# An attention level cut into a state step and a chunk step, in a fused attention and two-MLP kernel

## The chip, the cores and the metric

The kernel runs on one core of one Trainium2 chip. The metric is the device time of one launch in microseconds (us), as the median of several executions. The engines are called as in the profile: PE is TensorE's matmul, PEld its weight load, DVE is VectorE, ACT is ScalarE, POOL is GpSimd and SP is the engine that issues most DMAs.

## The reference

A gated linear attention over 4 batches, 8 heads and 768 positions (head size 32, state size 16) feeds two MLPs over 3072 tokens of width 256 and hidden width 2048.

```python
for c in range(nc):                      # chunks of the sequence
    cum = np.cumsum(la, axis=-1)         # la: log of the decays a
    M = einsum('bhin,bhjn->bhij', Cc, Bc) * exp(cum_i - cum_j) * causal
    y_intra = einsum('bhij,bhjd->bhid', M, xc)
    y_inter = einsum('bhin,bhnd->bhid', Cc, state) * exp(cum)
    y[:, :, sl] = y_intra + y_inter
    state = decay_full * state + sum_j(Bc * xc * decay_from_j)
...
x = relu(x @ w_in) ** 2 @ w_out          # first MLP
h = x @ w2_in
out = (h * clip(h + 3, 0, 6) / 6) @ w2_out
```

## The kernel before

The kernel is written with a manual schedule: each engine executes its instructions in the order in which the code emits them, and waits where an operand is not there yet.

The attention is cut into 12 levels of 64 positions. A level needs, on PE: `scores` (C times B for each head, 16 matmuls as written), `inter` (the state times C, 32 matmuls of 32 columns of weights each), `update` (the new contribution to the state, 16) and `intra` (the masked scores times x, 32). All four are in fp32, and each such matmul as written shows in the profile as two matmuls and two weight loads. They use one PSUM tile `att` per level, of which there is only one buffer. `phase(l)` emits, in one go, the scores of level l+1 and then inter, update and intra of level l. On the other engines a level has: `scale` (POOL, B and C times decays, L289), `heads` (ACT, the operand `cb` of the scores, L298), `tokens` (POOL, L304), `mask` (DVE, L323, reads the scores), `advance` (DVE, the next state S, L374 and L376, reads the part `u` of `att` that update wrote), `evac_h` (ACT, L389, the high part of the result, `act_h`) and `evac_l` (DVE, L394, the low part, `act_l`).

Levels 0 and 1 are done before the first MLP begins. The rest is done between the steps of the first MLP. There are 96 steps; a step takes one block of 128 hidden units for 512 tokens: `mm1` (6 matmuls into `ha`, L516), then a gate (relu on ACT, a square on ACT or a product on DVE, the high part `gha` on ACT, the low part `gla` on DVE), and the `mm2` (6 matmuls into `ya`, L550) of two steps before. `ORDER` gives the steps: tile 0 with 10 blocks, tile 1 with 10 blocks, then the rest. So step 10 is the first that needs the results of levels 2 and 3.

The table `PLAN` says which attention work is emitted in which step: for level l, phase in step 4l-5, then mask, advance, tokens and evac_h in step 4l-4, evac_l and scale in step 4l-3, heads in step 4l-2. Work on PE stands between `mm1` and `mm2` of its step, the other work after ACT's `gha` of its step. In the same steps the weights of the first MLP are decoded (`early` on ACT L433, `join` on DVE L437 to L447, `split` on ACT L474 and POOL L476, by the table `JOIN1`). The table `SQUARE` lists the steps whose square ACT does instead of DVE. `gammas` multiplies the decays of the later levels (3 instructions, in step 2). `keep_busy` issues dummy matmuls. Later come the second MLP's steps, from the line L656 on.

Of the kernel before, what the change touches and what calls it, by code (L numbers as in the profile page):

```python
# [8 lines left out]
F32 = mybir.dt.float32  # L9
# [5 lines left out]
ALU = mybir.AluOpType  # L15
# [3 lines left out]
P = 128  # L19
# [29 lines left out]
ORDER += [(t, f) for t in range(2, NT) for f in range(NF)]  # L49


PLAN = {0: ["adv1", "upd1", "head2"], 1: ["first2", "tok2", "scale3"], 2: ["mask2", "head3", "gammas0"]}
for _l in range(2, 12):
    for _k, _v in ((-1, ("load",)), (0, ("phase",)), (1, ("mask+", "adv", "tok+", "high")), (2, ("low", "scale++")),
                   (3, ("head++",))):
        PLAN.setdefault(4 * _l - 5 + _k, []).extend(
            f"{v.rstrip('+')}{_l + v.count('+') + 2 * (v == 'load')}" for v in _v)

JOIN1 = {0: 3, 1: 4, 2: 5, 3: 6, 5: 7, 6: 8, 7: 9, 10: 10, 11: 11, 14: 12, 15: 13, 18: 14, 19: 15}
DMA1 = {0: 6, 1: 7, 2: 8, 3: 9, 5: 10, 6: 11, 10: 12, 11: 13, 14: 14, 15: 15}

SQUARE = (1, 2, 3, 4, 5, 7, 8, 9, 10, 12, 14, 16, 18, 20)
QKEEP = 3
QNEW = 4

# [8 lines left out]
def attn_mlp_mlp(ctx: ExitStack, tc, a, bT, cT, bK, x, w1i, w1o, w2i, w2o, yT):  # L76
# [153 lines left out]
                          .unsqueeze(1).broadcast_to([H, NS, 2 * NGRP * CPG]))  # L230

    def gammas():
        nc.vector.tensor_tensor(out=gl[:, 1, :, 0:NLEV - 1], in0=gl[:, 1, :, 0:NLEV - 1], in1=gl[:, 0, :, 1:NLEV],
                                op=ALU.mult)
        for e in range(2):
            nc.vector.tensor_scalar(out=gam1[:, :, :, e].rearrange("p l b -> p b l"), in0=gl[:, 1, :, CPG - 1:NLEV - 1],
                                    scalar1=hm[:, e:e + 1], scalar2=None, op0=ALU.mult)

    def gamma(l):
        return gam0[:, l] if l < CPG - 1 else gam1[:, l - CPG + 1]  # L240
# [66 lines left out]
    def scores(l, sc):  # L307

        d = lev[l]
        d["s"] = sc  # L310
        for c in range(2):
            for p in range(NPR):
                for r in range(2):
                    q, b = slice(32 * p, 32 * p + 32), 2 * r + c
                    nc.tensor.matmul(out=sc[CH * r:CH * r + CH, p, P * c:P * c + P].rearrange("j (e i) -> j e i", e=2),  # L315
                                     lhsT=d["bc"][q, b, 1], rhs=d["cb"][q, :, b], start=True, stop=True)
# [7 lines left out]
                                      tri.bitcast(U32).unsqueeze(1).unsqueeze(1).broadcast_to([P, 2, NB, CH]),  # L324
                                      sc[:, q].rearrange("p k (z i) -> p k z i", i=CH))

    def inter(l, m=HD):

        y, d = lev[l]["y"], lev[l]
        for b in range(NB):  # L330
            for p in range(NPR):
                q, (r, c) = slice(32 * p, 32 * p + 32), divmod(b, 2)
                for e in range(0, 2 * HD, m):
                    o = CH * (p % 2) + e
                    nc.tensor.matmul(out=y[o:o + m, 2 * r + p // 2, c * CH:c * CH + CH],  # L335
                                     lhsT=state["S"][q, b, e:e + m], rhs=d["bc"][q, b, 0], start=c == 0,
                                     stop=False, skip_group_check=True)

    def intra(l):

# [13 lines left out]
    def update(l):  # L354

        if l == NLEV - 1:
            return
        u, x = lev[l]["u"], lev[l]["xb"]
        for c in range(2):
            for r in range(2):  # L360
                q = slice(CH * r, CH * r + CH)
                for p in range(NPR):
                    nc.tensor.matmul(out=u[32 * p:32 * p + 32, 2 * r, 2 * HD * c:2 * HD * c + 2 * HD],
                                     lhsT=x[q, c, DM + 32 * p:DM + 32 * p + 32], rhs=x[q, c, 64 * p:64 * p + 64],
                                     start=not l, stop=True, skip_group_check=True)
# [28 lines left out]
            nc.vector.tensor_tensor(out=lo, in0=outputs(l, r), in1=hi.bitcast(F32), op=ALU.subtract)  # L394

    def place(l, t):
        lev[l].update(t=t, y=t[:, :, G:G + P], u=t[:, :, G + P:])

    def phase(l):
        t = ps_a.tile([P, NPR, TOK], F32, tag="att", name=f"att{l}")  # L400
        place(l, t)
        if l + 1 < NLEV:
            scores(l + 1, t[:, :, 0:G])
        inter(l)
        update(l)
        intra(l)


    class Weights:
# [313 lines left out]
    def run(g, point):  # L723
        for f in jobs.pop((g, point), ()):
            f()
# [88 lines left out]
    ftps = ps_a.tile([P, NPR, TOK], F32, tag="att", name="ftp")  # L814
    f_tokens(0)
    f_tokens(1)
    keep_busy(4, ftps[:, 2])
    gammas_out()
    decays_out()
    gammas_in()  # L820
# [24 lines left out]
    update(0)  # L845
    keep_busy(2, lev[0]["t"][:, 3, 0:G], G)
    intra(0)
    load_x(3)
    advance(0)
    evac_h(0)  # L850
    evac_l(0)
    place(1, ps_a.tile([P, NPR, TOK], F32, tag="att", name="att1"))
    inter(1, 2 * HD)
    intra(1)
    w1.sign(1)
    w1.bits(1)
    evac_h(1)
# [12 lines left out]
    def first_scores(l):  # L870
        sc = ps_a.tile([P, NPR, TOK], F32, tag="att", name=f"att_s{l}")
        scores(l, sc[:, :, 0:G])

    does = {"load": load_all, "scale": scale, "head": heads, "tok": tokens, "first": first_scores, "mask": mask,
            "phase": phase, "high": evac_h, "low": evac_l, "upd": update, "adv": advance, "gammas": lambda _: gammas()}

    def attention(n, on_pe):
        for nm in PLAN.get(n, ()):
            k = nm.rstrip("0123456789")
            l = int(nm[len(k):])  # L880
            if (k in ("phase", "first", "upd")) == on_pe and (l < NLEV or k in ("load", "scale", "head")):
                does[k](l)

    todo = {}
# [14 lines left out]
            w1.early(plan[f + 1])  # L899

    def mid(n):
        attention(n, False)
        decode(JOIN1, n)
        if n in DMA1:
            w1.dma(DMA1[n])
        run(n, 0)


    for q, base in enumerate((48, 54, 60, 66, 72, 79, 86, 91)):
# [88 lines left out]
```

## Time and profile before

| | us |
|---|---|
| median of 3 runs (592.23 to 594.0) | 593.2 |
| the profiled execution, its own time | 590.14 |
| its span in the profile | 588.4 |
| PE busy | 557.6 |
| DVE busy | 420.8 |
| ACT busy | 361.1 |
| POOL busy | 141.7 |

The span is the time from the first to the last instruction of the profiled execution, and its own time is that with what lies around it. A busy share is an average over the whole span; which engine waits for which has to be read stretch by stretch.

### The profile page before, as it was taken

How to read it: one execution, taken by the hardware profiler on the slowest of the kernel's cores; microseconds unless marked ns; L12 is line 12 of the kernel's file. 1: busy time of each engine (PE TensorE's matmuls, PEld its weight loads, DVE VectorE, ACT ScalarE, POOL GpSimd, SP SyncE). 2: the span in 40 equal slices, each digit the busy share in tenths (PEclk: the TensorE clock that was granted, in tenths of full speed). 3: DMA queues.
4: the chain of work that ended last, by engine and by line, in shares of the span. 5: the costliest groups of instructions: out<-in, count | busy, mean ns of one | idle time of the engine just before them, and what ended most of it. 6: DMA issues, size and time to landing. Idle time of an engine off the chain costs nothing.

```text
span 588.4 us, 11061 instructions
## 1 busy us (share of the span) xinstructions
PE 557.6 (95%) x4451; PEld 450.4 (77%) x4451; DVE 420.8 (72%) x662; ACT 361.1 (61%) x629; POOL 141.7 (24%) x195
## 2 busy tenths in 40 slices
PE   7879998888899999999999899999999999999996
PEld 3557876777688888888887678888788888788885
DVE  6889787455654576677777877788776878777674
ACT  4567865443434556656665776687766777666663
POOL 5355443510000134444346500330000510000000
PEclk9789999999989999999999999999999999999999
DMA  8895442212000111222121000000200000200002
GB/s 245 210 263 139 125 135 81 78 37 90 1 2 1 36 43 65 73 71 72 41 66 38 1 1 0 1 1 1 72 1 0 1 2 0 71 2 0 1 1 72
DMA packets 26467, 31.47 MB, mean 53 GB/s; under 512 B 2128, under 2 KB 21040, under 8 KB 26416
## 3 DMA queue, kind: packets, MB, share of 16 engines
q1 hardware_dynamic: 24544, 29.85, 18.3%
q10 hardware_dynamic: 1872, 0.92, 0.6%
q8 instruction: 35, 0.57, 0.4%
q14 instruction: 16, 0.13, 0.1%
HBM read 27.41 MB, written 3.35 MB: 52 GB/s over the span
## 4 chain that ended last, share of the span: by engine, by line
PE 81%; issue 5%; POOL 4%; DVE 4%; DMA 2%; ACT 2%; SPq 1%; POOLq 0%; DVEq 0%; ACTq 0%
PE y L701 22%; PE ya L550 18%; PE ha L516 17%; PE X L656 11%; PE Z L656 6%; PE V L656 3%; PE att L349 1%; PE att L335 1%; POOL al L476 1%; PE att L315 1%; POOL bc L289 1%; DMA bc<-in_bT 1%; DMA gsc<-gs 1%; POOL wtb L456 1%; POOL bl L502 1%
## 5 line engine op out<-in xcount | busy, mean ns | idle before, releaser
L533 DVE TENSOR_TENSOR gla<-ga,gha 128x512 fp32r<-128x512 f32 x96 | 75.9, 791 | 41.0 <-ACT gha L531 40.5
L523 ACT ACTIVATE ga<-ha 128x512 f32<-128x512 f32 x96 | 57.3, 597 | 68.1 <-PE ha L516 67.8
L531 ACT ACTIVATE gha<-ga 128x512 fp32r<-128x512 f32 x96 | 60.6, 631 | 53.5 <-DVE ga L529 53.2
L529 DVE TENSOR_TENSOR ga<-ga,ha 128x512 f32<-128x512 f32 x82 | 56.2, 685 | 45.7 <-ACT ga L523 45.3
L550 PE MATMUL ya<-gla,ah 128*128 128x512 f32 x192 | 75.7, 394 | 1.4 <-DVE gla L533 1.4
L516 PE MATMUL ha<-act_h,ah 128*128 128x512 f32 x192 | 76.2, 397 | 0.7 <-ACT act_h L389 0.7
L550 PE MATMUL ya<-gha,ah 128*128 128x512 f32 x192 | 76.4, 398 | 0.2 <-ACT gha L531 0.2
L516 PE MATMUL ha<-act_h,al 128*128 128x512 f32 x192 | 75.7, 394 | 0.0
L550 PE MATMUL ya<-gha,al 128*128 128x512 f32 x192 | 75.3, 392 | 0.0
L516 PE MATMUL ha<-act_l,ah 128*128 128x512 f32 x192 | 75.2, 393 | 0.0
L687 DVE TENSOR_TENSOR glc<-c,ghc 128x512 fp32r<-128x512 f32 x96 | 67.6, 706 | 5.9 <-ACT ghc L684 4.7
L678 DVE SCALAR_TENSOR_TENSOR c<-rc,c 128x512 f32<-128x512 f32 x72 | 51.0, 708 | 23.7 <-ACT rc L670 23.4
L670 ACT ACTIVATE rc<-c,three 128x512 f32<-128x512 f32 x72 | 52.0, 722 | 24.5 <-DVE c L665 24.3
L701 PE MATMUL y<-ghc,bh 128*128 128x512 f32 x168 | 65.5, 390 | 0.0
L701 PE MATMUL y<-glc,bh 128*128 128x512 f32 x168 | 65.4, 389 | 0.0
L701 PE MATMUL y<-ghc,bl 128*128 128x512 f32 x168 | 65.4, 389 | 0.0
L684 ACT ACTIVATE ghc<-c 128x512 fp32r<-128x512 f32 x96 | 58.6, 629 | 3.4 <-DVE c L678 3.2
L665 DVE TENSOR_TENSOR c<-Z,u 128x512 f32<-128x512 f32 x48 | 33.1, 690 | 22.9 <-PE Z L656 22.1
L550 PEld LDWEIGHTS ya<-gla,ah 128*128 128x128 f32 x192 | 36.3, 189 | 10.6 <-DVE gla L533 3.1
L550 PEld LDWEIGHTS ya<-gha,ah 128*128 128x128 f32 x192 | 36.2, 189 | 10.4 <-issue 2.0
L516 PEld LDWEIGHTS ha<-act_h,ah 128*128 128x128 f32 x192 | 36.7, 191 | 8.9 <-ACT act_h L389 1.0
L661 ACT COPY u<-X 128x512 f32<-128x512 f32 x48 | 28.2, 588 | 24.4 <-PE X L656 24.3
(299 smaller groups left out, 1037.4 us busy)
## 6 DMA issues: line engine op xcount, KB each, us to landing
rawa<-in_w1i SPq DMA_DIRECT2D x8, 512.0 KB
rawa<-in_w1o SPq DMA_DIRECT2D x8, 512.0 KB
rawb<-in_w2i SPq DMA_DIRECT2D x8, 512.0 KB
rawb<-in_w2o SPq DMA_DIRECT2D x8, 512.0 KB
xb<-in_x SPq DMA_DIRECT2D x24, 128.0 KB
ef<-scr SPq DMA_DIRECT2D x10, 256.0 KB
out_yT<-xf SPq DMA_DIRECT2D x10, 256.0 KB
bc<-in_cT SPq DMA_DIRECT2D x6, 256.0 KB
```

Source lines behind the costliest of these rows:

```text
L516: nc.tensor.matmul(out=h, lhsT=wt[fb][:, k, fo * P:fo * P + P], rhs=xt[t][:, k, :], start=i == 0, stop=i == 5)
L523: nc.scalar.activation(out=g, in_=h, func=AF.Relu)
L529: nc.vector.tensor_tensor(out=g, in0=g, in1=h, op=ALU.mult)
L531: nc.scalar.activation(out=gh, in_=g, func=AF.Copy)
L533: nc.vector.tensor_tensor(out=gl, in0=g, in1=gh.bitcast(F32), op=ALU.subtract)
L550: nc.tensor.matmul(out=ys[m], lhsT=terms[i][0][fb][:, fo, m * P:m * P + P], rhs=terms[i][1], start=first and i == 0, stop=last and i == 2)
L656: nc.tensor.matmul(out=self.ps[bank], lhsT=lhsT, rhs=rhs, start=start and i == 0, stop=stop and i == 2, skip_group_check=True)
L670: nc.scalar.activation(out=self.sb["r" + c], in_=src, func=AF.Relu, bias=three)
L678: nc.vector.scalar_tensor_tensor(out=self.sb[c], in0=self.sb["r" + c], scalar=6.0, in1=src, op0=ALU.min, op1=ALU.mult)
L684: nc.scalar.activation(out=self.gh[c], in_=self.sb[c], func=AF.Copy)
L687: nc.vector.tensor_tensor(out=self.gl[c], in0=self.sb[c], in1=self.gh[c].bitcast(F32), op=ALU.subtract)
L701: nc.tensor.matmul(out=ys[t][m], lhsT=terms[i][0][:, 7 + 2 * (1 - f) + m], rhs=terms[i][1], start=first and i == 0, stop=last and i == 2, ...
```

## The change

`phase` is split in two. `from_state(l)` (inter and update) is emitted in step 4l-5, and `advance` in the same step; `from_chunk(l)` (intra of level l and the scores of level l+1) is emitted in step 4l-4. Mask, evac_h and evac_l all move to step 4l-3. `inter` uses 64 columns of weights a matmul, so 16 instead of 32. The `u` part of `att` now lies where the scores of level l+1 are written. The three instructions of `gammas` go from DVE to POOL (one) and ACT (two). There are 5 and 4 and 4 more dummy matmuls ahead of the first step. `SQUARE` gets steps 0 and 6 and loses step 20, and three steps of the decoding tables shift by one.

```diff
-    for _k, _v in ((-1, ("load",)), (0, ("phase",)), (1, ("mask+", "adv", "tok+", "high")), (2, ("low", "scale++")),
-                   (3, ("head++",))):
-        PLAN.setdefault(4 * _l - 5 + _k, []).extend(
+    for _k, _v in ((-2, ("load",)), (-1, ("state", "adv")), (0, ("chunk", "tok+")), (1, ("mask+", "high", "low", "scale++")),
+                   (2, ("head++",))):
+        PLAN.setdefault(4 * _l - 4 + _k, []).extend(
...
-SQUARE = (1, 2, 3, 4, 5, 7, 8, 9, 10, 12, 14, 16, 18, 20)
+SQUARE = (0, 1, 2, 3, 4, 5, 6, 7, 8, 9, 10, 12, 14, 16, 18)
...
     def gammas():
-        nc.vector.tensor_tensor(out=gl[:, 1, :, 0:NLEV - 1], in0=gl[:, 1, :, 0:NLEV - 1], in1=gl[:, 0, :, 1:NLEV],
+        nc.gpsimd.tensor_tensor(out=gl[:, 1, :, 0:NLEV - 1], in0=gl[:, 1, :, 0:NLEV - 1], in1=gl[:, 0, :, 1:NLEV],
                                 op=ALU.mult)
         for e in range(2):
-            nc.vector.tensor_scalar(out=gam1[:, :, :, e].rearrange("p l b -> p b l"), in0=gl[:, 1, :, CPG - 1:NLEV - 1],
-                                    scalar1=hm[:, e:e + 1], scalar2=None, op0=ALU.mult)
+            nc.scalar.activation(out=gam1[:, :, :, e].rearrange("p l b -> p b l"), in_=gl[:, 1, :, CPG - 1:NLEV - 1],
+                                 func=AF.Copy, scale=hm[:, e:e + 1])
...
-                for e in range(0, 2 * HD, m):
-                    o = CH * (p % 2) + e
-                    nc.tensor.matmul(out=y[o:o + m, 2 * r + p // 2, c * CH:c * CH + CH],
-                                     lhsT=state["S"][q, b, e:e + m], rhs=d["bc"][q, b, 0], start=c == 0,
-                                     stop=False, skip_group_check=True)
+                o = CH * (p % 2)
+                nc.tensor.matmul(out=y[o:o + CH, 2 * r + p // 2, c * CH:c * CH + CH], lhsT=state["S"][q, b],
+                                 rhs=d["bc"][q, b, 0], start=c == 0, stop=False, skip_group_check=True)
...
-        lev[l].update(t=t, y=t[:, :, G:G + P], u=t[:, :, G + P:])
-
-    def phase(l):
-        t = ps_a.tile([P, NPR, TOK], F32, tag="att", name=f"att{l}")
-        place(l, t)
-        if l + 1 < NLEV:
-            scores(l + 1, t[:, :, 0:G])
+        lev[l].update(t=t, y=t[:, :, G:G + P], u=t[:, :, 0:P])
+
+    def from_state(l):
+
+        place(l, ps_a.tile([P, NPR, TOK], F32, tag="att", name=f"att{l}"))
         inter(l)
         update(l)
+
+    def from_chunk(l):
+
         intra(l)
+        if l + 1 < NLEV:
+            scores(l + 1, lev[l]["t"][:, :, 0:G])
...
-    keep_busy(4, ftps[:, 2])
+    keep_busy(9, ftps[:, 2])
...
     intra(0)
+    keep_busy(4, lev[0]["t"][:, 3, 0:G], G)
...
     intra(1)
+    keep_busy(4, lev[0]["t"][:, 3, 0:G], G)
...
     def mid(n):
-        attention(n, False)
+        attention(n, False, "adv")
         decode(JOIN1, n)
         if n in DMA1:
             w1.dma(DMA1[n])
         run(n, 0)
+        attention(n, False, *(k for k in does if k != "adv"))
```

On PE, level 5 before stands in one piece, between the `ha` matmuls of step 15 and the `ya` matmuls behind it.

```order
L516 MATMUL ha_5_1264<-act_l_349,ah_533 128x512
L315 MATMUL att_1281<-cb_1246,bc_1016 64x128 x16
L335 MATMUL att_1281<-bc_555,S_1193 32x64 x32
L363 MATMUL att_1281<-xb_796 32x64 x16
L349 MATMUL att_1281<-mt_93,xb_796 32x64 x32
L550 MATMUL ya_00_1182<-gha_3_1208,ah_439 128x512
```

After the change the same level stands in two pieces; between them are the six `ya` matmuls of step 15 and the six `ha` matmuls of step 16 (the first and the last of them are shown).

```order
L517 MATMUL ha_5_1229<-act_l_358,ah_546 128x512
L334 MATMUL att_1246<-bc_568,S_1075 64x64 x16
L361 MATMUL att_1246<-xb_793 32x64 x16
L551 MATMUL ya_00_1139<-gha_3_1163,ah_453 128x512
...
L517 MATMUL ha_6_1296<-act_l_358,ah_665 128x512
L347 MATMUL att_1246<-mt_93,xb_793 32x64 x32
L315 MATMUL att_1246<-cb_1211,bc_997 64x128 x16
L551 MATMUL ya_00_1139<-gha_4_1199,ah_546 128x512
```

So the 96 matmuls as written that stood together became 32 and 48, and the scores went from the front of a level to its end, one step later.

On ACT, in step 2 and at the beginning of step 3, before: `cb` is the scores' operand for level 3, `wta` the next weights being decoded, `ga` the relu of step 3 and its square.

```order
L531 ACTIVATE gha_2_528<-ga_2_530 128x512
L298 ACTIVATE cb_549<-bc_211,hm 128x256 x2
L433 ACTIVATE wta_569<-rawa_474 128x512
L523 ACTIVATE ga_3_583<-ha_3_574 128x512
L525 ACTIVATE ga_3_583<-ga_3_583 128x512
```

And after the change, at the same place.

```order
L532 ACTIVATE gha_2_541<-ga_2_543 128x512
L298 ACTIVATE cb_562<-bc_216,hm 128x256 x2
L236 ACTIVATE gam_102<-gl,hm 128x4x8 x2
L434 ACTIVATE wta_582<-rawa_484 128x512
L524 ACTIVATE ga_3_596<-ha_3_587 128x512
L526 ACTIVATE ga_3_596<-ga_3_596 128x512
```

The two instructions of `gammas` now stand ahead of the decoding and of step 3's relu; they read `gl`, which POOL writes after two of its `al` instructions (L477).

On DVE, level 2 before, from step 4 to step 5: mask, advance, and one step later evac_l.

```order
L533 TENSOR_TENSOR gla_3_582<-ga_3_583,gha_3_581 128x512
L323 COPY_PREDICATED mt_93<-tri,att_589 128x512 x2
L374 TENSOR_TENSOR S_726<-att_589,S_462 128x256
L376 TENSOR_TENSOR S_726<-S_726,gam_101 128x256
L533 TENSOR_TENSOR gla_4_708<-ga_4_709,gha_4_707 128x512
L394 TENSOR_TENSOR act_l_349<-att_589,act_h_730 128x2x2x64 x2
```

After the change, from step 3 to step 5 (`lowa` and `wta` are a join).

```order
L448 SCALAR_TENSOR_TENSOR wta_582<-wta_582,lowa_642 128x512
L372 TENSOR_TENSOR S_649<-att_602,S_486 128x256
L374 TENSOR_TENSOR S_649<-S_649,gam_101 128x256
L534 TENSOR_TENSOR gla_3_595<-ga_3_596,gha_3_594 128x512
...
L534 TENSOR_TENSOR gla_4_661<-ga_4_662,gha_4_660 128x512
L323 COPY_PREDICATED mt_93<-tri,att_602 128x512 x2
L392 TENSOR_TENSOR act_l_358<-att_602,act_h_757 128x2x2x64 x2
```

Advance moved one step earlier and stands behind a join; mask moved one step later, next to evac_l.

## Rows read from the trace of the kernel before

**Rows 1.** Stretches: busy us (x instructions) by engine, PE's granted clock, DMA share, GB/s.
```profile
35.00:38.50 3.50, 3.45 (x188) 2.98 (x192) 3.33 (x6) 2.77 (x5) 1.19 (x3) 0.51 1.09 209
53.66:175.59 121.93, 111.51 (x1862) 89.53 (x1856) 78.40 (x127) 61.25 (x120) 30.51 (x38) 0.99 0.26 73
161.30:164.70 3.40, 3.40 (x9) 2.70 (x9) 0.00 (x0) 0.00 (x0) 0.00 (x0) 0.51 0.02 5
175.60:302.00 126.40, 126.40 (x563) 104.68 (x559) 85.00 (x132) 75.39 (x126) 41.02 (x58) 1.00 0.17 51
```

**Rows 2.** Waits of PE from 53.66 to 175.59: us in total, times, longest.
```profile
PE att L349 <- issue: 7.4, 5, 1.7
```

**Rows 3.** Timeline of PE at level 9: start, us, instruction, [idle before].
```profile
140.18 0.70 PE L315 MATMUL att<-cb,bc 32*64 32x128 f32 x32 [0.29 <-issue]
140.80 0.85 PE L335 MATMUL att<-bc,S 32*32 32x64 f32 x64
141.59 0.46 PE L363 MATMUL att<-xb 64*32 64x64 f32 x32
141.85 0.79 PE L349 MATMUL att<-mt,xb 64*32 64x64 f32 x50
144.08 0.34 PE L349 MATMUL att<-mt,xb 64*32 64x64 f32 x14 [1.44 <-issue]
```

**Rows 4.** Timeline of PE: the same place in levels 6 and 10.
```profile
96.88 0.79 PE L349 MATMUL att<-mt,xb 64*32 64x64 f32 x56 [1.71 <-issue]
...
161.19 0.21 PE L349 MATMUL att<-mt,xb 64*32 64x64 f32 x1 [1.74 <-issue]
```

**Rows 5.** Timeline of ACT and PEld; third row: a group, 53.66 to 175.59.
```profile
139.19 0.89 ACT L298 ACTIVATE cb<-bc,hm 128x256 f32<-128x256 f32 x2
140.15 0.38 PEld L315 LDWEIGHTS att<-cb,bc 32*64 32x64 f32 x24 [0.68 <-issue]
L315 PEld LDWEIGHTS att<-cb,bc 32*64 32x64 f32 x224 | 3.4, 131 | 5.6 <-issue 4.8 <-POOL bc L289 0.8
174.02 0.37 PEld L335 LDWEIGHTS att<-bc,S 32*32 32x32 f32 x34 [0.35 <-issue]
```

**Rows 6.** The chain that ended last, after level 8: start, us, what.
```profile
128.78 1.59 PE ya L550 x6
130.37 1.36 PE ha L516 x6
```

**Rows 7.** Timeline of PE: inter of level 1, with 64 columns.
```profile
16.69 0.50 PE L335 MATMUL att<-bc,S 32*64 32x64 f32 x17 [0.81 <-DVE S L376]
17.57 0.46 PE L335 MATMUL att<-bc,S 32*64 32x64 f32 x15 [0.39 <-issue]
```

**Rows 8.** Timeline of PE, DVE, POOL and ACT from 31 to 52.
```profile
35.05 1.16 PE L315 MATMUL att<-cb,bc 32*64 32x128 f32 x32 [3.73 <-ACT cb L298]
51.15 0.70 PE L315 MATMUL att<-cb,bc 32*64 32x128 f32 x32 [1.29 <-POOL al L476]
31.40 1.36 DVE L323 COPY_PREDICATED mt<-tri,att_s 128x512 f32<-128x512 uint32 x2
33.97 1.42 POOL L476 TENSOR_TENSOR al<-wta,ah 128x256 fp32r<-128x256 f32 x2
34.04 0.91 ACT L298 ACTIVATE cb<-bc,hm 128x256 f32<-128x256 f32 x2 [0.86 <-POOL bc L289]
38.69 0.50 PE L550 MATMUL ya<-gha,ah 128*128 128x512 f32 x1
```

**Rows 9.** Timeline of ACT in step 8: gate, then evac_h of level 3.
```profile
58.44 0.61 ACT L531 ACTIVATE gha<-ga 128x512 fp32r<-128x512 f32 x1
58.96 0.63 ACT L389 CAST act_h<-att 128x256 fp32r<-128x256 f32 x2
```

**Rows 10.** Timeline of PE: dummies before the first scores.
```profile
9.41 1.04 PE L792 MATMUL ftp<-idle 128*128 128x512 bf16 x4
12.45 1.21 PE L315 MATMUL att_s<-cb,bc 32*64 32x128 f32 x64 [2.00 <-ACT ft L214]
```

More of the change, by code (lines that the diff above doesn't have):

```diff
@@ L49 @@
 ORDER += [(t, f) for t in range(2, NT) for f in range(NF)]
-PLAN = {0: ["adv1", "upd1", "head2"], 1: ["first2", "tok2", "scale3"], 2: ["mask2", "head3", "gammas0"]}
+PLAN = {0: ["upd1", "adv1", "head2"], 1: ["first2", "tok2", "scale3"], 2: ["mask2", "head3", "gammas0"]}
 for _l in range(2, 12):
-    for _k, _v in ((-1, ("load",)), (0, ("phase",)), (1, ("mask+", "adv", "tok+", "high")), (2, ("low", "scale++")),
-                   (3, ("head++",))):
-        PLAN.setdefault(4 * _l - 5 + _k, []).extend(
+    for _k, _v in ((-2, ("load",)), (-1, ("state", "adv")), (0, ("chunk", "tok+")), (1, ("mask+", "high", "low", "scale++")),
+                   (2, ("head++",))):
+        PLAN.setdefault(4 * _l - 4 + _k, []).extend(
             f"{v.rstrip('+')}{_l + v.count('+') + 2 * (v == 'load')}" for v in _v)
-JOIN1 = {0: 3, 1: 4, 2: 5, 3: 6, 5: 7, 6: 8, 7: 9, 10: 10, 11: 11, 14: 12, 15: 13, 18: 14, 19: 15}
-DMA1 = {0: 6, 1: 7, 2: 8, 3: 9, 5: 10, 6: 11, 10: 12, 11: 13, 14: 14, 15: 15}
-SQUARE = (1, 2, 3, 4, 5, 7, 8, 9, 10, 12, 14, 16, 18, 20)
+JOIN1 = {0: 3, 1: 4, 2: 5, 3: 6, 4: 7, 6: 8, 7: 9, 10: 10, 12: 11, 14: 12, 15: 13, 18: 14, 20: 15}
+DMA1 = {0: 6, 1: 7, 2: 8, 3: 9, 5: 10, 6: 11, 10: 12, 12: 13, 14: 14, 15: 15}
+SQUARE = (0, 1, 2, 3, 4, 5, 6, 7, 8, 9, 10, 12, 14, 16, 18)
 QKEEP = 3
@@ L325, in mask, with inter @@
                                       sc[:, q].rearrange("p k (z i) -> p k z i", i=CH))
-    def inter(l, m=HD):
+    def inter(l):
         y, d = lev[l]["y"], lev[l]
@@ L852, in attn_mlp_mlp @@
     place(1, ps_a.tile([P, NPR, TOK], F32, tag="att", name="att1"))
-    inter(1, 2 * HD)
+    inter(1)
     intra(1)
+    keep_busy(4, lev[0]["t"][:, 3, 0:G], G)
     w1.sign(1)
@@ L874, in attn_mlp_mlp, with attention @@
     does = {"load": load_all, "scale": scale, "head": heads, "tok": tokens, "first": first_scores, "mask": mask,
-            "phase": phase, "high": evac_h, "low": evac_l, "upd": update, "adv": advance, "gammas": lambda _: gammas()}
-    def attention(n, on_pe):
+            "state": from_state, "chunk": from_chunk, "high": evac_h, "low": evac_l, "upd": update, "adv": advance, "gammas": lambda _: gammas()}
+    def attention(n, on_pe, *without):
         for nm in PLAN.get(n, ()):
             k = nm.rstrip("0123456789")
+            if k in without:
+                continue
             l = int(nm[len(k):])
-            if (k in ("phase", "first", "upd")) == on_pe and (l < NLEV or k in ("load", "scale", "head")):
+            if (k in ("state", "chunk", "first", "upd")) == on_pe and (l < NLEV or k in ("load", "scale", "head")):
                 does[k](l)
```

## The prediction, written before the changed kernel ran

> **What bounds the kernel now.** I read the stretches first, then PE's waits in the stretch that the change touches, then one level instruction by instruction, and last what each wait ends on.
>
> The stretches [rows 1] show two different kernels. From 175.6 to 302 PE is busy without a gap, and whatever comes before only shifts it. From 53.66 to 175.59, where levels 4 to 11 lie between the MLP's steps, PE is busy 111.5 of 121.9 us. A us taken from PE's path ahead of 175 is therefore a us off the end. Steps themselves are at their limit: six matmuls take 1.36 us [rows 6], a step 2.72, four steps 10.88. What can go is what a level costs beyond that: 121.93/8 - 10.88 = 4.4 us on average.
>
> Of this, 7.4 us over the eight levels is PE waiting in the middle of `intra` (L349) for nothing that the profile shows [rows 2]. Level 9 shows where [rows 3]: scores, inter, update and 50 of intra's 64 matmuls run densely in about 2.5 us, then PE stands still for 1.44 us, then the last 14 run. The same happens in levels 6 to 10, five times. In level 6 there are 56 matmuls behind the gap and in level 10 one [rows 4]; between them the count falls by 14 a level (42, 28, 14). So the place is not tied to an operand. A level issues 192 small and 48 large matmuls, each with a weight load, 480 instructions, and the gap comes 14 pairs later each level, which is every 508 instructions. A stop at fixed distances in the instruction stream, with no semaphore behind it, reads as instructions that have not arrived. It shows when many instructions run in a short time, as in these bursts of 384 in 2.5 us. Level 5 has none: there its place comes early in the burst, and the slow matmuls before gave time to fetch ahead.
>
> The Trainium skill ("Runtime: NRT & Kernel Launch", Instruction fetch mechanics) says that an engine's instructions are refilled in blocks of 256 while the current one executes, and that crossing a block is mostly hidden. The spacing of 508, two such blocks, agrees; the hidden cost does not, with 1.2 to 1.7 us in five levels. By that sentence the gaps would be something else and the first term below would be 0; this is my first rival.
>
> Two smaller costs stand beside it. Every level's scores begin when ACT has finished their operand: in level 9 `cb` ends at 140.08 and the weight load starts at 140.15 [rows 5]. Heads come one step ahead of the scores, and ACT's relu, DVE's product and ACT's `gha` stand ahead of them, so they are always a little late. And after level 10's gap PE's clock falls to the lower of its two levels, 0.51 granted for 3.4 us [rows 1].
>
> **The change part by part.**
>
> *The split.* A dense piece is now 48 matmuls as written (192 instructions) or 32 (128), with 24 instructions of 2.72 us between. Any 256 instructions in a row now contain at least these 24, so they take over 4 us (192 dense in 1.5, 24 in 2.72, 40 more in 0.2) where the old burst took 256 in 1.7. A refill that came 1.2 to 1.7 us late there takes up to 3.4, and is hidden behind the large matmuls. I count all five gaps: **-7.4**. If it took over 4.4, part would come back; the bound is 0.
>
> *The clock after level 10.* No pause, no fall: 3.4 x 0.49 = **-1.7** (bound 0).
>
> *Scores one step later.* The seven entries of scores (levels 4 to 10) hold 5.6 us of idle weight loads [rows 5]. Level 11, which has no scores, enters with 0.35; I take that as the entry without a wait: 5.6 - 7 x 0.35 = **-3.1**. After the change `cb` has a whole step and the state piece more, so it is not late. The new first instruction, inter, needs S (a level old), and `att` free. Mask, evac_h and evac_l of the level before end some 3.5 us after their step's `mm1` (product to 1.35, mask 1.36, evac_l 0.75), and PE gets to inter 5.4 us after it: 2 us to spare.
>
> *Inter with 64 columns.* 64 profile matmuls took 0.79 from start to start [rows 3]. Level 1 ran this form [rows 7]: 17 in 0.50 and 15 in 0.46; less a lone matmul's 0.2 as tail each, 32 take 0.56. Bounds: 0.40 if a matmul costs the same in both forms, 0.79 if it costs double. 0.23 x 8 = **-1.8** (0 to -3.1).
>
> *One more entry and exit a level.* The `ya` matmuls behind a burst take 1.59 instead of 1.36 [rows 6], 0.23 for the exit. An entry costs between 0 and the 0.35 of level 11; I take 0.1, since the loads in steady state also leave small gaps. 0.33 x 8 = **+2.6** (1.8 to 4.6). In the order, PE changes between shapes of matmuls 6 times a level instead of 4; what that would cost at a higher price is a rival below. The Trainium skill ("TensorEngine Tiling (Array Packing)", Key Properties) says that a change of tiling mode drains TensorE, which speaks against this change; the rows give such a change a small price, 0.1 to 0.3 us.
>
> *The first ten steps (levels 2 and 3).* Waits that go: PE stood 3.73 us for level 3's `cb`, until 35.05 [rows 8]. Now state(2) needs only that mask(2) has read its tile, at 32.7: -2.2. The 1.29 at 51.15 goes with the later scores: -1.3. The phase from 35.05 to 38.69 ran at a granted clock of 0.51 after the long pause [rows 1], in 3.6 us instead of 2.5: -1.1 if the shorter pause keeps the clock. Given back: ACT waits for `gl`, which POOL writes after `al` (33.97 to 35.39). gl is nearest to half of that row's two (0.7 each, four times as many elements; 0.1 to 0.7, I take 0.3), each gam nearest to a `cb` instruction (0.45; I take 0.25 for a quarter of the elements). So ACT goes on at 36.2 instead of 34.9, and early and relu of step 3, split and `gha` behind it are 1.3 late. Advance(2) stands behind a join that waits for that early, and the scores now write where advance reads u: PE +0.7 (0 to 2). `mm1` of step 8 waits for a split that ACT and POOL do in order behind all this: +1.0 (0 to 2). `mm1` of step 10 needs `act_h` of level 3, which moved to step 9: relu, square, `gha` and the cast, 0.6 each [rows 9], 2.5 after step 9's `mm1`, against 1.36 of `ya`: +1.1. Entries and exits of two levels: +0.7. Sum **-1.1** (-4.6 to +3). What DVE gains (`gammas`, two products) is not in it, since the path there runs over ACT and POOL.
>
> *Dummies.* Four of 512 columns took 1.04 us [rows 10], and PE then stood idle 2.00 until the scores. Five more take 1.3 and end before. The two fours of 256 columns take about 0.5 each and lie in pauses of 0.8 [rows 7] and 0.7. If they keep the clock up from 18 to 25, PE is faster there, but step 2 goes on when mask(2) is done, and that hangs on ACT and POOL. **0** (-2 to +0.5).
>
> *Other moves.* Decoding steps that shift by one, tokens, scale and loads: each is needed 2 or more steps later. The buffer of x is freed one step later, and its next use is three levels away. 0.
>
> **Sum:** -7.4 - 1.7 - 3.1 - 1.8 + 2.6 - 1.1 = -12.5. The profiled execution's 590.14 becomes 577.6; the median stands 3.1 above that execution, so I predict **580.7**. Its own range, from the bounds of the small terms, is 575 to 584.
>
> **The rivals.**
>
> *The gaps stay.* If they are no late refill, or come back in another place, -7.4 and -1.7 fall away: -3.4, 589.8. For it: the profile names no cause. Against: the step of 14 a level and no gap in levels 4 and 5. Chance 0.12.
>
> *The first ten steps lose.* ACT's wait for POOL and the later evac_h cost their upper bounds: +3 instead of -1.1, 584.8. For it: DVE, ACT and POOL are all near full there. Chance 0.14.
>
> *Changes of shape cost more.* This ends slower: PE has two more of them in each of levels 2 to 11, 20 in all. Without my term for them (2.6 + 0.7) the sum is -15.8, so the sign turns where one costs 0.8 us; at 1.0 it is 597.4. For it: level 9's entry took 0.68. Against: there `cb` was late, and 0.35 is all that level 11 shows. Chance 0.03.
>
> *Scores wait for advance.* The new overlap of u and scores: PE reaches them about 5 us after `mm1` of the state's step, DVE is done with u after 2 to 3. A join in between makes it close in early levels only. At 2 us in each of 10 levels: +20 - 12.5, 600.7. Chance 0.02.
>
> **How the numbers follow.** My forecast holds 0.69, with a tail on either side. The range of 574 to 588 takes in the second rival and the bounds of the terms, and leaves out most of the first and both slow ones. This kernel's measurement can tell about 0.3%, 1.8 us, from no change. Forecast, second and nearly all of the first rival are faster: 0.92; 0.03 within; 0.05 slower.
>
> **What would show it.** PE's wait on L347 (now intra) without a releaser should be gone, PEld's idle at L315 near 0.35 or less a level, and the stretch from level 3's end to level 11's near 110 us. Inter's 32 matmuls take 0.56. The granted clock is 1.0 through the levels. ACT waits for POOL at L236; step 10's `ha` waits for `act_h`. Wrong would be: such gaps in other places, waits of PE on DVE's L372, or entries of 0.6 and more without a named releaser.

## The result and the profile after

The changed kernel takes 582.81 us, median of 4 runs (582.18 to 583.82); the kernel before took 592.72 beside it (590.45 to 594.0). The ratio is 0.9839 with an interval of 0.9804 to 0.9873: faster, by 9.9 us. The prediction was 580.7 with a range of 574 to 588. The profiled execution took 582.18 with a span of 580.5, against 590.14 and 588.4 before: 7.9 us less.

Three stretches of the changed kernel: until level 3's `intra` and scores are done (56.89), levels 4 to 11 (to 170.38), and the rest. Columns as in [rows 1].

```profile
0.00:56.89 56.89, 47.68 (x787) 31.93 (x787) 43.66 (x80) 34.77 (x72) 31.12 (x48) 0.91 0.81 220
56.89:170.38 113.49, 110.15 (x1609) 85.94 (x1601) 73.30 (x125) 60.93 (x117) 27.88 (x36) 1.00 0.25 71
170.38:580.50 410.12, 401.16 (x1763) 328.98 (x1758) 297.68 (x453) 266.60 (x444) 84.55 (x112) 1.00 0.09 26
```

The middle row answers to 53.66:175.59 in [rows 1]: eight levels and 32 steps in both. It fell from 121.93 to 113.49, by 8.44 us. They end one step apart, though: the changed kernel's first stretch reaches to the `mm2` of step 8, and that of before to the `mm2` of step 7. In the profile of before the `mm2` of step 8 begins at 56.55, so the start lost 0.3. What follows step 40 takes 409.9 to 410.1 us in every profile of this study. The whole difference therefore lies in two numbers, the place of step 8 and the length of steps 8 to 40, and I use these two for all experiments.

PE's waits in the middle stretch. Before, there were these three rows beside the one of [rows 2]:

```profile
PE att L315 <- issue: 2.3, 5, 0.9
PE att L315 <- POOL bc L289: 0.4, 1, 0.4
PE ya L550 <- ACT gha L531: 0.2, 1, 0.2
```

After:

```profile
PE att L347 <- DVE S L372: 2.0, 2, 1.8
PE ha L517 <- ACT act_h L387: 1.2, 1, 1.2
```

The 7.4 us without a releaser are gone, and so are the waits ahead of the scores (L315). Waits with a releaser have come, in levels 5 and 8 and ahead of step 10's `mm1`, 3.2 us together. Level 9 on PE, which answers to [rows 3]:

```profile
138.19 0.69 PE L334 MATMUL att<-bc,S 32*64 32x64 f32 x32
138.82 0.45 PE L361 MATMUL att<-xb 64*32 64x64 f32 x32
...
142.19 0.86 PE L347 MATMUL att<-mt,xb 64*32 64x64 f32 x64
142.98 0.69 PE L315 MATMUL att<-cb,bc 32*64 32x128 f32 x32
```

Both pieces run through. `inter` takes 0.63 from start to start where it took 0.79. Weight loads in the same stretch, by group: busy and mean ns, then idle time ahead of them with what ended it. They answer to the third row of [rows 5]:

```profile
L347 PEld LDWEIGHTS att<-mt,xb 64*32 64x32 f32 x512 | 5.6, 105 | 5.1 <-DVE S L372 3.4 <-issue 1.4 <-DVE S L374 0.4
L334 PEld LDWEIGHTS att<-bc,S 32*64 32x64 f32 x256 | 4.5, 132 | 2.9 <-issue 2.9
L315 PEld LDWEIGHTS att<-cb,bc 32*64 32x64 f32 x224 | 3.2, 131 | 0.6
```

Scores now enter with 0.6 us in all instead of 5.6. The entries have moved to `inter`, 2.9 in eight levels where it was 1.6, and to `intra`, 1.4 without the waits for DVE.

The new wait in level 5, first on PE, then on DVE:

```profile
86.74 0.86 PE L347 MATMUL att<-mt,xb 64*32 64x64 f32 x64 [1.76 <-DVE S L372]
```

```profile
83.74 0.98 DVE L438 TENSOR_SCALAR lowa<-rawa 128x512 uint32<-128x512 uint32 x1
84.76 0.87 DVE L443 TENSOR_SCALAR lowa<-rawa 128x512 uint16<-128x512 uint16 x1
85.66 0.69 DVE L448 SCALAR_TENSOR_TENSOR wta<-wta,lowa 128x512 uint32<-128x512 uint32 x1
86.27 0.41 DVE L372 TENSOR_TENSOR S<-att,S 128x256 f32<-128x256 f32 x1
```

Step 15 decodes a weight block, and the join's three instructions now stand ahead of `advance`. PE, back after 2.7 us of wide matmuls, stands until `advance` has read u. `intra` writes another part of the same tile; why it has to wait for that reading the profile does not say. It is not the new place of u: in e2 below, where u lies apart from the scores, `intra` waits for `advance` too. The smaller wait, in level 8, has no join ahead of `advance`, but two additions of `ya` results (L561, 1.28).

The start, first on ACT, then on PE:

```profile
11.73 0.48 ACT L214 COPY ft<-ftp 64x96 f32<-64x96 f32 x2 [1.17 <-PE ftp L793]
...
37.26 0.58 ACT L236 ACTIVATE gam<-gl,hm 128x32 f32<-128x32 f32 x2 [1.35 <-POOL gl L233]
```

```profile
9.58 2.12 PE L793 MATMUL ftp<-idle 128*128 128x512 bf16 x9
13.70 1.32 PE L315 MATMUL att_s<-cb,bc 32*64 32x128 f32 x64 [2.00 <-ACT ft L214]
...
28.95 1.16 PE L315 MATMUL att_s<-cb,bc 32*64 32x128 f32 x32 [2.98 <-POOL al L477]
...
39.83 0.86 PE L347 MATMUL att<-mt,xb 64*32 64x64 f32 x64 [0.31 <-DVE S L372]
...
62.47 0.50 PE L517 MATMUL ha<-act_h,ah 128*128 128x512 f32 x1 [1.19 <-ACT act_h L387]
```

The nine dummies write the tile that ACT copies `ft` from, so the copy waits for them, and the scores, which wait for the copy, begin 1.25 us later than in [rows 10]. The pause of 2.00 was not theirs to fill: it moved with them.

### The profile page after: what moved, and what is told of

Read it like the earlier page. It is cut to its first block, busy times and chain, and to the rows that moved or that the text cites. A ratio compares the mean times of both kernels' runs of the same rounds, so it can differ in the third digit from the quotient of the medians.

```text
span 580.5 us, 10441 instructions
## 1 busy us (share of the span) xinstructions
PE 559.0 (96%) x4144; PEld 446.8 (77%) x4144; DVE 414.6 (71%) x658; ACT 362.3 (62%) x632; POOL 143.6 (25%) x196
## 4 chain that ended last, share of the span: by engine, by line
PE 78%; DVE 6%; DMA 5%; ACT 3%; issue 3%; POOL 3%; SPq 1%; ACTq 0%; DVEq 0%; POOLq 0%
PE y L702 23%; PE ya L551 16%; PE ha L517 16%; PE X L657 11%; PE Z L657 6%; DMA ef<-scr 3%; PE V L657 3%; DMA rawa<-in_w1o 1%; PE att L347 1%; DVE ga L530 1%; ACT ga L524 1%; PE att L315 1%; POOL wtb L457 1%; DMA scr<-efr 1%; DVE mt L323 1%
## 5 line engine op out<-in xcount | busy, mean ns | idle before, releaser
L503 POOL TENSOR_TENSOR bl<-wtb,bh 128x256 fp32r<-128x256 f32 (+1 forms) x42 | 34.9, 865 | 34.2 <-ACT bh L496 29.8
```

## The experiments

Times are medians; ratios are to the kernel before, run beside each. Nothing is left out of the computation in any of them.

**e1 and e1b: move the place of the stops.** The kernel before, with 14 or 7 tiny dummies more in the prologue.

```
     keep_busy(13, big[:, 0])
+    ...
+    keep_busy(14, big[:, 0, 0:CH], CH)      # e1; 7 in e1b
```

> The kernel before, with 14 more tiny dummy matmuls (64 columns, 28 instructions of TensorE) behind the first 13 in the prologue; nothing else. Theory (TensorE's instructions come in blocks at fixed counts, and a burst of short ones outruns the supply): the place of the 1.0 to 1.7 us stop inside a level hangs on the count of instructions since the start, so it moves 14 matmuls towards the front: behind the stop, intra has 56 matmuls left in level 7, 42 in level 8, 28 in level 9, 14 in level 10 where the kernel before has 56 in level 6 and so on down to 1 in level 10, and level 6 has its stop before the first matmul of intra. The time stays within 0.5% of before. Rival (the stop hangs on an operand that comes late, or on a place in the level): the stops stay where they were, at 56 left in level 6, 42, 28, 14 in levels 7, 8, 9 and 1 in level 10.

> The kernel before with 7 more tiny dummies (14 instructions of TensorE) in the prologue instead of 14. Theory (fixed counts): the stops move by 7 matmuls, so 49 of intra are left in level 7, 35 in level 8, 21 in level 9 and 8 in level 10. For level 6, whose place would be 63 left, behind 129 short matmuls (258 instructions) of the burst: the kernel before has a stop behind 136 (1.71 us), the one with 14 dummies none behind 122. If a burst must use up one block of 256 instructions before it can stop, level 6 stops 1 to 1.7 us here; if it takes 130 or more matmuls, it does not. Rival (bound to an operand): the places of before.

e1 took 589.98 and e1b 596.15, one run each. The timeline of e1 on PE, levels 6 (no stop) and 7, against [rows 4]:

```profile
95.74 0.90 PE L349 MATMUL att<-mt,xb 64*32 64x64 f32 x64
...
111.82 0.79 PE L349 MATMUL att<-mt,xb 64*32 64x64 f32 x56 [1.62 <-issue]
```

The timeline of e1b on PE, levels 6 to 10:

```profile
98.55 0.85 PE L349 MATMUL att<-mt,xb 64*32 64x64 f32 x63 [1.80 <-issue]
...
116.06 0.73 PE L349 MATMUL att<-mt,xb 64*32 64x64 f32 x49 [1.47 <-issue]
...
133.99 0.85 PE L349 MATMUL att<-mt,xb 64*32 64x64 f32 x35 [1.67 <-issue]
...
151.59 0.42 PE L349 MATMUL att<-mt,xb 64*32 64x64 f32 x21 [1.79 <-issue]
...
168.66 0.32 PE L349 MATMUL att<-mt,xb 64*32 64x64 f32 x8 [1.66 <-issue]
```

Before, 56, 42, 28, 14 and 1 matmuls were left behind the stop in levels 6 to 10. With 7 dummies it is 63, 49, 35, 21, 8; with 14 it is 56, 42, 28, 15 in levels 7 to 10. The stop moves by the number of added instructions and by nothing else: the rival that ties it to an operand falls. Where e1's theory was too simple is level 6, which has no stop at all with 14 dummies. There the place lies behind 122 short matmuls of the burst (244 instructions); behind 129 (258) and 136 (272) there was one of full length. By these counts the burst has to have used up 244 to 258 instructions before it can stop.

The trace also holds the transfers of the instructions. The page lists the DMA queues with packets, MB and share of the DMA engines' time, and one of kind `instruction` goes by TensorE's count, first before, then after the change:

```profile
q8 instruction: 35, 0.57, 0.4%
q8 instruction: 32, 0.52, 0.4%
```

A packet is 16 KB. There are 35 for 8902 counted instructions of TensorE (matmuls and weight loads) and 32 for 8288, so 254 to 259 in each. The same list for a short window shows when a packet begins. This is the only instruction packet from 94.50 to 95.50 in the profile of before, 0.93 us of one DMA engine's time:

```profile
q8 instruction: 1, 0.02, 5.8%
```

Such windows, narrowed to 0.02 us, give for each level the packet that belongs to its stop:

| | level 6 | level 7 | level 8 | level 9 | level 10 |
|---|---|---|---|---|---|
| before: the packet begins | 94.61 | 110.35 | 126.06 | 141.72 | 158.60 |
| before: the stop ends | 96.88 | 112.65 | 128.34 | 144.08 | 161.19 |
| e1: the packet begins | 91.74 | 109.49 | 125.63 | 141.25 | 158.26 |
| e1: the stop ends | no stop | 111.82 | 127.91 | 143.75 | 160.88 |
| e1b: the packet begins | 95.90 | 113.73 | 131.17 | 149.16 | 166.06 |
| e1b: the stop ends | 98.55 | 116.06 | 133.99 | 151.59 | 168.66 |

In all 14 stops the packet begins inside the burst, 1.0 to 1.8 us behind its first matmul, and the stop ends 2.3 to 2.8 us after that. In level 6 of e1 it begins 2.3 us ahead of the burst (94.06), among wide matmuls, and no stop follows. So a stop is a block of instructions that comes late. The 28 added instructions moved this packet's start by 3.8 us against the burst, and 14 moved it by 0.5: that is why the stop vanished and did not shrink. What sets the start is not shown.

e1b's 596.15 shows a second cost. Its stretches behind the stops of levels 6, 7, 8 and 9 (the granted clock is the third number from the right):

```profile
100.00:102.00 2.00, 2.00 (x6) 1.57 (x5) 1.61 (x4) 0.00 (x0) 0.00 (x0) 0.50 0.19 53
...
117.00:119.00 2.00, 2.00 (x6) 1.54 (x6) 0.00 (x0) 0.00 (x0) 0.00 (x0) 0.50 0.75 223
...
135.00:137.00 2.00, 2.00 (x5) 1.59 (x6) 0.54 (x1) 0.00 (x0) 0.00 (x0) 0.50 0.15 41
152.00:154.00 2.00, 2.00 (x10) 1.66 (x10) 0.00 (x0) 0.00 (x0) 0.00 (x0) 1.00 0.03 8
```

After three of the stops the clock went to the lower level, and the six `ya` and six `ha` behind them took 4.45, 4.46 and 4.01 us instead of 2.85. In the profile of before that happened once, behind level 10 [rows 1]. The stops themselves were 1.0 us longer in sum (8.4 instead of 7.4), and step 8 began at 58.32 instead of 56.55.

**e2: the split alone.** The kernel before with `phase` cut in two and its table of steps; `inter` in 32 columns, u's place, gammas, dummies, joins and the order in a step stay those of before.

```
-    for _k, _v in ((-1, ("load",)), (0, ("phase",)), (1, ("mask+", "adv", "tok+", "high")), (2, ("low", "scale++")),
+    for _k, _v in ((-2, ("load",)), (-1, ("state", "adv")), (0, ("chunk", "tok+")), (1, ("mask+", "high", "low", "scale++")),
```

> The kernel before with the split alone: state products and update in step 4l-5, intra and the next scores in step 4l-4. The 32-column inter, u's place, the gammas on VectorE, the dummies, the tables of joins, squares and loads, and the order of advance, decode and the rest in a step are those of before. Theory (the stops in the dense levels are what the change takes away): 9 us (7 to 11) faster than before, about 583 to 586, no stop of over 0.5 us inside a level. Rival (the 64-column inter and the rearranged first steps bring it): within 2 us of before.

583.75 (581.09 to 584.02), ratio 0.9835 [0.9795, 0.9875]: as much as the whole change. Steps 8 to 40 take 112.85 us, and this is all that PE waits for in them:

```profile
PE ha L519 <- ACT act_h L389: 1.2, 1, 1.2
PE att L349 <- DVE S L374: 0.4, 1, 0.4
```

The split is the gain: 9.1 us of its 121.93 in this stretch. Everything else in the change nets to nothing that this measurement tells.

**e3: without the added dummies.**

```
-    keep_busy(9, ftps[:, 2])
+    keep_busy(4, ftps[:, 2])
...
-    keep_busy(4, lev[0]["t"][:, 3, 0:G], G)
...
-    keep_busy(4, lev[0]["t"][:, 3, 0:G], G)
```

> The changed kernel with the dummies of before: four instead of nine at the tokens, none behind intra of level 0 and level 1. Theory (the dummies stand on the path at the start and hold nothing that is used later): mm1 of step 0 begins 2 to 2.5 us earlier; the end comes 0.3 to 2 us earlier, since step 2's scores and step 4 wait for VectorE either way. Rival (they hold the clock at a level that the first steps need): the stretch to step 4 is 0.5 to 2 us longer at a lower granted clock, and the end as much later.

581.93 (580.97 to 583.77), ratio 0.9822 [0.9794, 0.9849]. `mm1` of step 0 begins at 20.25 instead of 22.34, 2.1 us earlier, and the gain at the end (0.9 to 1.3 by medians) is within the spread of the runs. The clock fell to its lower level in all three profiles: from 18 to 25 before, 16 to 22 after, 14 to 23 without the added ones. That is not so in each profile, though. From 14 to 23 the mean granted clock was 0.62 in this profile of the changed kernel, but 0.81 (e0), 0.81 (e4), 1.00 (e5) and 1.00 (e7) in the others with the added dummies, and 0.50 to 0.86 in the seven with those of before. Whether they help to hold the clock stays open; the time does not gain by them.

**e4: advance ahead of the join.**

```
-        attention(n, False, "adv")
+        attention(n, False)
         decode(JOIN1, n)
         ...
-        attention(n, False, *(k for k in does if k != "adv"))
```

> The changed kernel with advance back among the other vector work ahead of the join (the order that the kernel before has) in all steps. Theory (advance behind the join is what makes TensorE stand 3 us before scores of level 2, and 1.8 us in level 5): scores of level 2 begin 2 to 3 us earlier, the waits of intra for advance in levels 2, 5 and 8 (0.3, 1.8, 0.2 us) are gone, and the end comes 2 to 4 us earlier than in the changed kernel. Rival (the join that then stands behind advance makes the split or mm1 of the next step late): within 1 us of the changed kernel or up to 2 us slower, with new waits of mm1 for ah or al.

581.11 (580.46 to 582.77), ratio 0.981 [0.9782, 0.9838]. Of the waits in steps 8 to 40 the 1.8 of level 5 is gone, and 0.6 of level 8 stays, more than the 0.2 it was:

```profile
PE ha L517 <- ACT act_h L387: 1.2, 1, 1.2
PE att L347 <- DVE S L372: 0.6, 1, 0.6
```

The stretch takes 112.11 instead of 113.49. Scores of level 2 came 2.0 earlier (26.98), but step 8 began at 58.91, 2.0 later; in this execution a weight block landed late. First e4, then the kernel e9b told below, on ACT:

```profile
28.91 0.68 ACT L434 ACTIVATE wta<-rawa 128x512 f32<-128x512 f32 x1 [2.03 <-DMA rawa<-in_w1i]
```

```profile
27.03 0.67 ACT L437 ACTIVATE wta<-rawa 128x512 f32<-128x512 f32 x1 [1.13 <-DMA rawa<-in_w1i]
```

In the two profiles of the changed kernel step 8 came at 56.89, without this wait, and at 59.26, with one until 29.17 (e0). Across the other versions the end of this wait and the place of step 8 mostly go together: 27.03 and 55.39 (e9b), 27.27 and 55.59 (e10), 27.29 and 56.12 (e3), 28.09 and 56.58 (e7), 28.91 and 58.91 (e4), 29.47 and 59.28 (e2), 29.60 and 58.69 (e9a); 27.04 and 58.41 (e5) does not fit. Of this spread of almost 4 us at least 2.4 come without any edit, so one profile says little of the first ten steps.

**e0: the changed kernel again, and e10: both halves in one step, with mm2 between.** e10 is e2 with this edit:

```
-    for _k, _v in (... (-1, ("state", "adv")), (0, ("chunk", "tok+")), ...
+    for _k, _v in (... (-1, ("state", "chunk", "adv")), (0, ("tok+",)), ...
...
-            attention(ORDER.index((t, f)), True)
+            attention(ORDER.index((t, f)), True, "chunk")
         if len(pend) == LAG:
             mm2(*pend.pop(0))
+        if t <= LASTATT:
+            attention(ORDER.index((t, f)), True, *(k for k in does if k != "chunk"))
```

> The changed kernel once more, unaltered, on the same chip as the next three. Both theories: 582.8 (582 to 584), 9.5 to 10 us under before; its first stretch (to mm2 of step 8) varies by 2 us from run to run with the landing of the weights, the rest by under 0.2 us.

> The split alone, as in the kernel of that run, but both halves in one step: state products and update ahead of mm2's six wide matmuls (1.4 us), intra and the next scores behind them, all in step 4l-5. Theory (the next block of instructions is only late: time between the bursts is what the split gives): the stops of 1.2 to 1.7 us in levels 6 to 10 are gone or under 0.4 us each, and the time is within 2 us of the split over two steps, 582 to 586. Rival (what counts is the number of short matmuls near each other, with or without 1.4 us between, so a full step of 2.7 us is needed): stops of 0.5 to 1.7 us remain in three or more of the five levels, and the time is 587 to 590.

e0: 583.24 (582.27 to 586.53), ratio 0.9832 [0.9804, 0.986]. Its steps 8 to 40 were not the same within 0.2 us, as I had expected, but 115.47 instead of 113.49: behind the wait of level 5 the clock fell, which it had not done in the other profile of the same kernel.

```profile
90.00:92.00 2.00, 2.00 (x36) 1.48 (x36) 1.28 (x2) 0.00 (x0) 2.00 (x3) 0.52 1.00 340
92.00:94.00 2.00, 2.00 (x7) 1.62 (x6) 0.00 (x0) 0.00 (x0) 1.83 (x3) 0.63 0.97 257
```

e10: 581.32 (580.39 to 583.76), ratio 0.9811 [0.9782, 0.9839]. Its timeline on PE, level 7:

```profile
108.23 0.45 PE L363 MATMUL att<-xb 64*32 64x64 f32 x32
108.62 0.50 PE L553 MATMUL ya<-gha,ah 128*128 128x512 f32 x1
...
110.20 1.11 PE L349 MATMUL att<-mt,xb 64*32 64x64 f32 x64
111.24 0.69 PE L315 MATMUL att<-cb,bc 32*64 32x128 f32 x32
```

The waits of 1.2 to 1.7 us are gone, with all 192 small matmuls in one step. A rest is seen: `intra` takes 1.04 to the next line instead of 0.79 here, 1.20 in level 8, and scores 1.13 instead of 0.63 in level 10, each without an idle row on PE. The stretch is 113.57, against 112.85 with the halves a step apart. This rest is the same stop, shortened. The weight loads pause for 0.2 to 0.3 us in these three places, with 48, 34 and 7 small matmuls left in the burst, about 14 fewer a level, and go on 2.5 to 2.6 us after an instruction packet began (108.40 and 110.97, 122.83 and 125.36, 151.90 and 154.36). The wide matmuls, here 1.6 us from 108.62 to 110.20, cover the remainder, and so they do nearly all that a whole step does. The rival falls.

**e9b and e9a: take the waits that are left.** e9b is the changed kernel with the edits of e3 and e4, and

```
+for _k in ("high3", "low3"):
+    PLAN[9].remove(_k)
+    PLAN[8].append(_k)
```

In e9a, moreover, `mask` of level 2 stands behind the join of step 1 instead of in step 2.

> The changed kernel with the dummies of before, advance ahead of the join in all steps, and the outputs of level 3 copied out one step earlier (in step 8, behind its intra). Theory (each of these three takes a wait that the trace of the changed kernel shows): the wait of step 10's mm1 for act_h (1.2 us) and that of intra in level 5 (1.8 us) are gone, the rest of step 8 to 40 stays, 110.6 us for those instead of 113.5; the end comes 2 to 4 us earlier than in the changed kernel run beside it. Rival (VectorE or ScalarE has no room in step 8: the copies make the mask of level 4 or the gate late): step 10 starts no earlier, and the time is within 1.5 us of the changed kernel.

> The kernel of the early copy, with the mask of level 2 in step 1 instead of step 2, behind the join of step 1. Theory (state products of level 2 wait for this mask, since the masked scores lie in the buffer that they need: in the run with advance first they begin 0.1 us behind its end, 2.0 us late): state(2) begins 1.5 to 2 us earlier and step 8's mm2 up to 2 us earlier. Rival (the first steps go by VectorE's joins and the landing of the weights, so PE only waits elsewhere): state(2) earlier, but mm2 of step 8 within 0.5 us of where it is without this edit.

e9b: 579.28 (576.98 to 581.39), ratio 0.9771 [0.974, 0.9801], 4.0 us under the changed kernel beside it. Steps 8 to 40 take 109.81, and what PE waits for in them is

```profile
PE att L350 <- DVE S L375: 0.2, 1, 0.2
```

The stretch became 3.7 us shorter where the rows of the changed kernel named 3.2 of waits. e9a: 579.62 (578.91 to 580.29), ratio 0.9777 [0.9749, 0.9805], with the same 109.81. Its weight block landed at 29.60, and state(2) began at 34.62 instead of 33.24 without a wait for the mask; the edit can't be told from the landing, and stays open.

**e11: that weight block's load earlier.** e9b with

```
     load(2)
+    w1.dma(4)
     load_x(2)
     load_ef(3)
-    w1.dma(4)
```

> The kernel with the early copy (dummies of before, advance first, level 3 copied out in step 8), and in the prologue the load of weight block 4 issued behind B and C of level 2 and ahead of that level's x and of level 3's decays, instead of behind them. Theory (what varies from run to run, and what step 8's place hangs on, is the landing of this block: in seven profiles ScalarE waits for it until 27.0 to 29.6 us, and step 8 follows at 55.4 to 59.3): no wait for it is left, mm2 of step 8 begins at 54 to 56 in every profile, the median is 577 to 578.5, and the runs lie within 2 us of each other. Rival (its landing goes by the DMA load at that time, whatever the order, or the other loads become late in its stead): the wait stays or moves to x of level 2 or the decays, and the median is 578.5 to 580.

577.62 (576.49 to 579.54), ratio 0.9741 [0.9703, 0.978], the fastest version here. But not as the theory has it: the wait for block 4 is gone, and ACT waits for block 5 instead, while step 8 begins at 57.22.

```profile
31.41 0.67 ACT L437 ACTIVATE wta<-rawa 128x512 f32<-128x512 f32 x1 [2.12 <-DMA rawa<-in_w1o]
```

The runs still spread over 3 us, and the interval overlaps e9b's. Whether this edit brings anything is not shown.

**e7: inter in 32 columns, and e5: gammas on VectorE.** Each is the changed kernel with this one part undone.

```
-            nc.scalar.activation(out=gam1[:, :, :, e]...   # e5: gl and gam back to nc.vector
+            nc.vector.tensor_scalar(out=gam1[:, :, :, e]...
...
-                nc.tensor.matmul(out=y[o:o + CH, ...   # e7
+                for e in range(0, 2 * HD, m):
+                    nc.tensor.matmul(out=y[o:o + m, ...
```

> The changed kernel with the state products of levels 2 to 11 in 32 columns again (64 matmuls instead of 32). Theory (the rows: 32 wide ones take 0.62 us, 64 narrow ones 0.79): 0.15 to 0.2 us longer in each of levels 3 to 11, 1.3 to 1.6 us in all, about 584.3; a level without a wait takes 13.93 to 13.95 us instead of 13.79. Rival (the burst of 64 and 32 short matmuls outruns the supply of instructions too, or the clock): stops of 0.5 us or more inside the state burst in some levels, 586 or more.

> The changed kernel with the three gamma operations back on VectorE. Theory (they are off the path on either side): within 1 us of the changed kernel, 582 to 584. Rival (VectorE's 2.1 us in step 2 come where advance and the joins are late): advance of level 2 ends 2 us later, intra of level 2 waits 2 us longer, and the end comes 1 to 2 us later.

e7: 585.47 (583.06 to 589.04), ratio 0.9871 [0.9827, 0.9916]. Its stretch is 114.63, 1.1 us more; a level without a wait takes 13.92 to 13.94 instead of 13.79. No stops: the theory holds, with 1.1 us for the term in this stretch. The median lies between its 584.3 and the rival's 586, with runs spread over 6 us. e5: 584.24 (583.69 to 587.15), ratio 0.9866 [0.9811, 0.9921]. The stretch is unchanged, 113.47. At the start `intra` of level 2 waits 2.68 for `advance` (0.31 and 2.06 in the two profiles of the changed kernel), and step 8 comes at 58.41 although the weight block was there at 27.04. That is the rival's mechanism, at 1 us by medians; it is not resolved from nothing.

## Why the prediction was right, and where its sum was off

**The gaps: right.** The -7.4 is there in full, and the cause is now shown by more than the old trace: the place goes by the count of instructions (e1, e1b), every stop ends 2.3 to 2.8 us after a transfer of instructions that began inside the burst, and either of two separations of the burst removes it (e2, e10). The reason given for level 5 holds too: its packet began at 75.02, 4.2 us ahead of the burst at 79.21. The first rival falls. The Trainium skill ("Runtime: NRT & Kernel Launch", Instruction fetch mechanics) speaks of blocks of 256 instructions and of crossings that are mostly hidden. The block agrees with the 254 to 259 counted instructions of a packet; the stops of 1.2 to 1.8 us show that such bursts are the exception.

**Clock, scores, inter, entries: right as a sum.** With the gaps I had -11.4 for levels 4 to 11, which makes 110.5 of 121.93. Measured are 113.49 with 3.2 of waits in it, 110.3 without; e9b, where all but 0.2 of the waits are gone, has 109.8. The clock's -1.7 was 1.6: the twelve wide matmuls behind level 10's stop took 4.44 where 2.85 is usual. `inter` was mis-sized (-1.8; e7 shows -1.1, and 32 matmuls take 0.63 and not 0.56). What is left for scores and entries is 1.5, where I had 0.5.

**The wait of step 10's mm1 for act_h: right,** 1.19 against +1.1.

**"Scores wait for advance ... a join in between makes it close in early levels only": this step failed.** I priced it as a rival at 0.02 and put nothing into the sum for levels 4 to 11 (0.7 for level 2). The join in between is what happens in level 5. It is `intra` that waits and not the scores, 2.0 us in two levels, and in e0 it took 1.6 more through the clock. The order of the two kernels showed `advance` behind `decode`; I took it as free. The sum was -12.5 and the span fell by 7.9; of the 4.6 us that are missing, 2.0 are here.

**"Dummies ... Five more take 1.3 and end before": wrong.** They end later than the old ones, and ACT's copy waits for them; scores and `mm1` of step 0 came 1.25 and 2.5 us late. At the end this is worth 1 us or nothing (e3).

**"The first ten steps -1.1": not confirmed.** Without the act_h wait it was -2.2; the profile shows +0.3, which is another 2.5 of the 4.6. ACT's wait for `gl` was as forecast (1.35 against 1.3), but the scores of level 2 waited 2.98 us. The row names POOL's `al`; `advance`, behind the join of step 0, had read their tile only 0.3 us before that ended, and with `advance` ahead of the join (e4) they began 2.0 earlier. How much that cost is covered by the landing of the weights.

**The offset of 3.1 failed too, to the other side.** By their own times the profiled execution gained 8.0 and the median 9.9, because the profiled execution stands only 0.6 under the median now. So the sum missed by 4.5 us and the offset by 2.4 the other way; that 580.7 lies 2.1 from 582.81 is in part luck. A part of the old distance can be the clock: each stop may be followed by half speed or not, 1.2 to 1.6 us each, and e1b paid three times where before's profile paid once. That the timed runs of before differ by this was not seen in them, and the landing of the weights adds its own spread.

## What to carry to other kernels

A wait without a releaser whose place moves by a constant from one round to the next should be tested by adding a few dummy instructions at the program's start: if it moves by that number, break the dense burst up with wide matmuls, before touching operands. The instruction queue in the list of DMA transfers, window by window, then shows whether a block was on its way. When a piece of work is cut in two, look at what stands between them on the other engines: the second half waits for the first half's reader, and a decode that has moved ahead of it is then on the path. Split a kernel's time at points behind which all versions agree, here steps 8 and 40, and a run-to-run spread in one stretch no longer hides an edit in another.

## What the runs showed of the hardware that I had not expected

- The profile shows instruction blocks as packets of 16 KB, one for 254 to 259 counted instructions of TensorE, 0.9 us of one DMA engine's time in the packet ahead of level 6's stop. A stop ended 2.3 to 2.8 us after its packet began.
- A burst of short matmuls stopped only where the boundary lay behind 129 or more of them (258 instructions); behind 122 (244) there was no stop, not a shorter one. From 129 on its length, 1.2 to 1.8, did not grow with the place: 1.80 behind 129, 1.71 and 1.62 behind 136, 1.74 behind 191.
- Pauses of nearly the same length did and did not cost the clock: behind 1.80, 1.47 and 1.67 us in e1b the granted clock was 0.50, behind 1.79 and 1.66 it stayed at 1.00; the same wait of 1.76 and 1.77 in two executions of the changed kernel left it at 1.00 once and at 0.52 once.
- Six wide matmuls, 1.6 us, in a burst of 384 instructions removed stops that had been 1.2 to 1.7 us long, and left 0.25 to 0.5 us of slower matmuls in three levels.
